# A gated attention and GeGLU kernel: the probabilities' product moved behind a down chain, and the ones' product moved behind the second sum

## The chip, the core and the metric

The kernel runs on one core of a Trainium2 chip. The metric is the device time of one execution in microseconds (us). Before the change three runs gave 1596.64, 1601.48 and 1602.04 us; the median is 1601.48 us.

TensorE is called PE below, VectorE DVE, ScalarE ACT, GpSimd POOL, and SyncE, which issues the transfers, SP.

## What is computed

For 2048 tokens of width 576, the output is a gated sum of two branches: `g * attention(x) + (1 - g) * ffn(x)`, with `g = sigmoid(x · gate_w)`.

- The attention branch has 32 heads of width 18 and works on four segments of 512 tokens. In each segment it takes a masked softmax of the scores and multiplies the probabilities by the values. It mixes this with what a running memory gives (a linear attention over the segments before), and the result goes through `wo`.
- The other branch is `(gelu(x @ w_gate) * (x @ w_up)) @ w_down`, with 4608 hidden columns. It is most of the work.

All of it is wanted in fp32 accuracy. The kernel writes each fp32 operand as two fp16 words, a high and a low one, and multiplies high by high, high by low and low by high.

## The kernel before

A first stage projects the queries, keys and values (up to about 255 us). Then comes a loop of 72 steps, `step(v)`, to about 1480 us, and last the product with `wo`.

The loop runs over 18 blocks `fb` of 256 hidden columns. A block takes four steps, `i4` = 0 to 3: two tiles `f` of 128 columns, each with the token pairs `p` = 0 and 1 (two segments of 512 tokens each). A step works out the gate sum and the up sum of its tile for two segments. It does so with fewer products than four, by a scheme of sums and differences: accumulators X in bank G, Y in bank U and V in bank V are filled by `product` and `rest`, copied and added by DVE, and end in `gelu` and `hidden`. In every block but the first, the steps with `i4` < 2 are the nested ones: their product into V is again split (`nest`, `nest_product`, `nest_last`), and its parts are spread over the step before.

Beside this, each step carries parts of other work:

- `chains` and `down`: the down products of the block before. A chain is six matmuls into a bank `dn`, over the two tiles of that block: hidden words (`hhr`, `hhd`) times the weight words `paird`. DVE adds the result to `acc` (line 1264). A step has eight chains, five `early` and three `late`.
- attention, two heads' halves a step: `scores` puts four score tiles into banks (tags `st`, `st`, `dn`, and `pv` or `dn`). DVE reads each with the mask and takes its maximum (line 1174, called by `put`). `powers` takes exponentials on ACT (line 1190), the high word on ACT (1191), the low word on POOL (1192), and has SP transpose both words by DMA into `pt`. `values` (line 1209) multiplies `pt` by the values: 20 small matmuls into bank `pv`.
- preparing the next weights: ACT makes high words, POOL low words. `low_d` (line 402) makes the low words of `paird` for a block in the last step of that block. `scales` multiplies the weights' sums of squares by a matrix of ones (two fp32 matmuls, line 94) and works out scales from them.

The order on PE, DVE, ACT and POOL is the order in which the code is written (`manual_schedule`); each engine runs its instructions in that order, and semaphores hold an instruction until its inputs are there and its output bank is free. The eight banks of PSUM are taken up by `dn` (two buffers), `st` (two), `pv`, V, G and U. A tag with two buffers hands them out in turn, so a third tile waits for the readers of the first.

At the end of a step stand `scores(2 * k + 1)`, whose last two tiles are both of tag `dn`, and, before a nested step, `nest(at, 3)`. The next step begins with `end_pair()`, in which DVE reads these two `dn` tiles, and then (lines 1454 to 1462):

```
            elif i4 < 2:
                if on(k - 2):
                    values(2 * k - 3)
                V, g1 = nested[fb, p], gl_tile()
            ...
            X, Y = bank("G"), bank("U")
            product(X, f, A11, x1, 0, 4, True)
```

Of the kernel before, what the change touches and what calls it, by code (L numbers as in the profile page):

```python
# [43 lines left out]
def kernel(ctx: ExitStack, tc: tile.TileContext, xs, wqk, wv, wo, wgu, wd, beta, out):  # L44
# [8 lines left out]
    def bank(tag, bufs=1, dt=F32):  # L53
        return ps.tile([P, 512 if dt == F32 else 1024], dt, name=tag, tag=tag, bufs=bufs)
# [36 lines left out]
    def sums(st, o=None):  # L91

        o = (spare() if o is None else o)[:, : st.shape[1]]
        pe.matmul(o, ones, st, start=True, stop=True)
        return o
# [168 lines left out]
    def scales(fb, o=None):  # L264

        o = sums(stat[fb % 2].rearrange("p a b -> p (a b)"), o)
        z = wts.tile([P, 6], F32, name="z", tag="z", bufs=2)
        dve.tensor_reduce(z[:, 4:6], o.rearrange("p (a b) -> p a b", a=2), AX.X, OP.add)
        dve.tensor_scalar(z[:, 0:4], x2, z[:, 4:5], 1e-30, OP.mult, OP.max)
        v = wts.tile([P, 2, 2], F32, name="v", tag="v", bufs=2)  # L270
        pb = wts.tile([P, 2, 4], F32, name="pb", tag="pb", bufs=3)
        dve.tensor_scalar(v[:, 0].bitcast(I32), z[:, 4:6].bitcast(I32), 1, EXP, OP.logical_shift_right, OP.bitwise_and)
        dve.tensor_scalar(pb[:, 0].bitcast(I32), z[:, 0:4].bitcast(I32), EXP, None, OP.bitwise_and)
        dve.tensor_scalar(v[:, 1].bitcast(I32), v[:, 0].bitcast(I32), EXP, None, OP.bitwise_xor)
        dve.tensor_scalar(pb[:, 1].bitcast(I32), pb[:, 0].bitcast(I32), EXP, None, OP.bitwise_xor)
        scl_a[fb] = v, pb

    def scales_out(fb):
        v, pb = scl_a.pop(fb)
        sc = wts.tile([P, 10], F32, name="sc", tag="sc", bufs=3)  # L280
        pool.tensor_scalar(sc[:, 0:2], v[:, 1], 2.0**-51, None, OP.mult)
        pool.tensor_scalar(sc[:, 2:6], xis, v[:, 0, 0:1], 2.0**50, OP.mult, OP.mult)
        pool.tensor_scalar(sc[:, 6:10], pb[:, 1], 2.0**14, None, OP.mult)
        pool.tensor_tensor(sc[:, 6:10], sc[:, 6:10], sc[:, 2:6], OP.mult)
        if fb:
            w = wts.tile([P, 4], F32, name="we", tag="we", bufs=2)
            pool.tensor_scalar(w, scl[fb - 1][1][:, 0], v[:, 0, 1:2], 2.0**35, OP.mult, OP.mult)
            ev = wts.tile([P, 16], F32, name="ev", tag="ev", bufs=2)
            pool.tensor_tensor(ev.rearrange("p (c q) -> p c q", c=4),
                               gate[:, 1].rearrange("p (c q) -> p c q", c=4),  # L290
                               w.unsqueeze(2).to_broadcast([P, 4, 4]), OP.mult)
            evs[fb - 1] = ev
        scl[fb] = (sc, pb)
# [167 lines left out]
    def nest_x(p):  # L461
        t = flat(kept["xt"][p][:, 8:15])
        return t[:, : 7 * HX], t[:, 7 * HX :]
# [13 lines left out]
    def nest_pairs_x(p, half):  # L477
        r, sc = sums_x[p][1, 2], xsc[:, 2 * p : 2 * p + 1]
        hi, lo = (t[:, 3 * HX :] for t in nest_x(p))
        if half == 0:  # L480
            act.activation(hi, r, AF.Copy, scale=sc)
        else:
            dve.scalar_tensor_tensor(lo, r, sc, hi, OP.mult, OP.subtract)
# [40 lines left out]
    def gl_tile():  # L524
        return mp2.tile([P, L], F32, name="gl", bufs=3)

    def product(o, f, a, x, h, l, start=False):

        w = pair_g[f]
        for k in range(2):  # L530
            for i, b in ((0, h), (0, l), (1, h)):
                pe.matmul(o, w[:, i, (a + k) * P : (a + k + 1) * P], x[:, b + k],  # L532
                          start=start and k == 0 and i == 0 and b == h, stop=k == 1 and i == 1,
                          skip_group_check=True)
# [3 lines left out]
    def first_product(v):  # L538
        f, p = divmod(v, 2)
        V = bank("pv" if v == 3 else "V")  # L540
        w = flat(s3_first["t"])
        for k, b in ((0, X00), (1, X10)):
            for i, j in ((0, 0), (0, 1), (1, 0)):
                a = (4 * i + 2 * f + k) * P
                x = nest_x(p)[j][:, b * HX : (b + 2) * HX]
                pe.matmul(V, w[:, a : a + P], x, start=k == i == j == 0, stop=k == i == 1, skip_group_check=True)
        if v == 3:
            s3_first.pop("t")
            hh_free.append(s3_first.pop("slot"))
        g1 = gl_tile()  # L550
        dve.tensor_copy(g1, V)
        return V, g1

    first, stay = ExitStack(), ctx.enter_context(ExitStack())
    with tc.tile_pool(name="prj", bufs=2, side="right", reuse_waits="tile") as pp:
# [135 lines left out]
        def vrows(s, q, b):  # L691
            x = x16[s]
            n = NH + 2 * b
            pv = bank("U") if (q, b) == (1, 0) else bank("dn", 2)
            chain_x(pv[:, :n], lambda i: x[:, i, q * P : (q + 1) * P], lambda k, i: W[9 + k][:, i, VB[b]])
            return pv, 2.0**-14, al[:, s, 1:2]
# [110 lines left out]
        with tc.manual_schedule(engines=ORDERED):  # L807
# [210 lines left out]
            for s in range(4):  # L1018
                p = s - 1
                if s:  # L1020
                    for q in range(4):
                        pv = vrows(s, q, 0)
# [14 lines left out]
                        pv = vrows(s, q, 1)  # L1037
# [67 lines left out]
    with tc.tile_pool(name="keep", bufs=2, side="right", reuse_waits="tile") as kp, ExitStack() as tail:  # L1105
# [91 lines left out]
        def values(a):  # L1197
            kk, e = divmod(a, 2)
            if e == 0:
                pvb[kk] = bank("pv")  # L1200
            o = pvb[kk]
            pr = turned_p.pop(a)
            v = vts[kk // 4]
            c0 = (kk % 4) * VC
            for qi in range(4):
                ov = o[:, (4 * e + qi) * VC : (4 * e + qi + 1) * VC]
                for kb in range(qi + 1):
                    for i in range(2):
                        pe.matmul(ov, pr[:, 10 * i + COL[qi] // P + kb], v[:, 4 * e + kb, c0 : c0 + VC],  # L1209
                                  start=kb == 0 and i == 0, stop=kb == qi and i == 1)  # L1210
# [19 lines left out]
        def result_high(gg):  # L1230
            ob = obs[gg]
            oh = ohs[gg] = ap_.tile([P, 8, 4 * DH], F16, name="oh", bufs=1)
            act.activation(flat(oh), flat(ob), AF.Copy, scale=wsc[:, 3:4])
# [32 lines left out]
        def chains(b, js):  # L1266
            for j in js:
                down(b, j // 2, j % 2)
                if j % 8 == 7:
                    for ff in (2 * b, 2 * b + 1):  # L1270
                        hp.pop((ff, j // 8))
                        hh_free.append(hh_slot.pop((ff, j // 8)))
                        if j == 31:
                            pair_d.pop(ff)
# [131 lines left out]
        def nest_last(b, V, p):  # L1406
            nest_product(b, V[:, HX : 2 * HX], WS4, X11, p)
# [20 lines left out]
        def step(v):  # L1428

            f, p = divmod(v, 2)  # L1430
            fb, i4 = divmod(v, 4)
            c, e = 2 * p, 2 * p + 1
            k = v - LAG
            on = lambda i: 0 <= i < 2 * H
            early = range(8 * i4, 8 * i4 + 5)
            late = range(8 * i4 + 5, 8 * i4 + 8)
            some = lambda b, js: chains(b, js) if b >= 0 else None
# [14 lines left out]
            if not fb:  # L1452
                V, g1 = ahead.pop(v) if v in ahead else first_product(v)
            elif i4 < 2:
                if on(k - 2):
                    values(2 * k - 3)
                V, g1 = nested[fb, p], gl_tile()
            else:
                V, g1 = bank("V"), holds[p]
                product(V, f, A22, x2_, 0, 4, True)  # L1460
            X, Y = bank("G"), bank("U")
            product(X, f, A11, x1, 0, 4, True)
            one = (2 if fb and i4 < 2 else 1) + (v == 4)
            if v == 4:
                dve.tensor_copy(Y, X)
                nest((1, 0), 2)
                some(0, early[:2])
                nest((1, 0), 3)
                some(0, early[2:3])
                nest_last(fb, V, p)  # L1470
                dve.tensor_copy(g1, V)  # L1471
                nest_pairs_x(1, 1)
            elif fb and i4 < 2:
                nest_last(fb, V, p)
                dve.tensor_copy(g1, V)
                dve.tensor_copy(Y, X)
                put(2 * k - 1, 3)
            else:
                put(2 * k - 1, 3)
                dve.tensor_copy(Y, X)  # L1480
# [5 lines left out]
                nest_pairs_x(v - 2, 0)  # L1486
            if v == 1:
                scale_result()
            some(fb - 1, early[3 * (v == 4) : one])
            put(2 * k - 1, 2)  # L1490
            puts.pop(2 * k - 1, None)
            if on(k - 2) and not (fb and i4 < 2):
# [62 lines left out]
                dve.tensor_tensor(g0, V, g0, OP.add)  # L1555
                gelu(f, c, g0, g0)
            put(2 * k, 0)
            some(fb - 1, early[3:])
            put(2 * k, 3)
            if fb and i4 == 1:  # L1560
                scales(fb + 1, bank("pv") if on(k) else None)
                scales_out(fb + 1)
            if on(k - 2) and not on(k):
                normalize(k - 2)
            if not fb:
# [7 lines left out]
            if done is not None:  # L1573
                result_high(done)
            product(Y, f, S4, x2_, 2, 6)
            if v == 3:
                nest(at, 1)
            rest(Y, f, UG, x2_, (0,) if fb else (0, 1))
# [184 lines left out]
        with tc.manual_schedule(engines=ORDERED):  # L1763
# [17 lines left out]
            fb = NB - 1  # L1781
# [88 lines left out]
```

## Time and profile before

| | |
|---|---|
| median of three runs | 1601.48 us |
| the profiled execution, its own time | 1598.08 us |
| its span | 1596.4 us |
| PE busy | 1564.9 us, 98% |
| DVE, ACT, POOL busy | 1249.5, 1208.7 and 1127.1 us |
| mean granted clock of PE | 0.996 |

PE is busy in nearly the whole span, so the time can only change where PE stands still or runs slower. A block of four steps takes some 74 us in the middle of the loop. The profile's timeline has one row for each group of like instructions, with the start, the duration, the engine, the line, and, in brackets, how long the engine had been idle before it and what released it. Where matmuls follow each other, the duration of a group contains the draining of its last one; the next group's start tells when PE could go on.

### The profile page before, as it was taken

To read this page: it belongs to the slowest core of one execution; us is meant where nothing else is said; L and a number is where in the kernel's file an instruction comes from. 1 tells how busy PE (TensorE), PEld (TensorE's weight loads), DVE (VectorE), ACT (ScalarE), POOL (GpSimd) and SP (SyncE) were. 2 spreads that over 40 slices of the span, in tenths; PEclk is the share of its full clock that TensorE was granted. 3 is DMA by queue.
4 is the path that set the end of the run, shared out by engine and by line. 5 is a ranking of instruction groups with operands and counts; after the bars stand their busy time and mean duration, and the time that the engine had idled before them with its cause. 6 is when DMAs were issued, how large, how long until landed. Compare 5 with 4: busy or idle time off the path is not lost.

```text
span 1596.4 us, 33958 instructions
## 1 busy us (share of the span) xinstructions
PE 1564.9 (98%) x12220; PEld 955.9 (60%) x12220; DVE 1249.5 (78%) x3254; ACT 1208.7 (76%) x2059; POOL 1127.1 (71%) x1220
## 2 busy tenths in 40 slices
PE   9999999999999999999999999999999999999999
PEld 5665655565555555556655555665555556656577
DVE  6788976778787788878887878888778888787665
ACT  7567544888888888888888888888878888787421
POOL 4345555877786858686786777776858686777597
PEclk9999999999999999999999999999999999999999
DMA  6534331676867767777767887868678767764546
GB/s 232 211 126 134 123 116 56 114 140 120 151 122 143 132 117 132 133 131 133 128 125 127 122 142 125 145 125 156 133 118 136 130 137 137 130 113 96 119 82 172
DMA packets 472833, 209.97 MB, mean 132 GB/s; under 512 B 427688, under 2 KB 437416, under 8 KB 472152
## 3 DMA queue, kind: packets, MB, share of 16 engines
q1 hardware_dynamic: 472664, 207.80, 65.5%
q8 instruction: 96, 1.57, 0.4%
q14 instruction: 73, 0.60, 0.1%
HBM read 91.87 MB, written 27.26 MB: 75 GB/s over the span
## 4 chain that ended last, share of the span: by engine, by line
PE 76%; DMA 7%; POOL 6%; DVE 5%; ACT 4%; issue 2%; SPq 0%; ACTq 0%; DVEq 0%; POOLq 0%
PE dn L1256 19%; PE U L532 14%; PE G L532 10%; PE V L532 5%; DMA pt<-pb 5%; PE pv L1209 4%; PE V L1377 3%; PE st L412 3%; PE dn L419 2%; POOL pb L1192 2%; PE U L1302 2%; PE U L412 1%; PE G L412 1%; PE V L1307 1%; PE st L1171 1%
## 5 line engine op out<-in xcount | busy, mean ns | idle before, releaser
L1192 POOL TENSOR_TENSOR pb<-pb,ph 128x896 f16<-128x896 f32 (+1 forms) x256 | 368.4, 1439 | 278.4 <-ACT ph L1191 268.4
L532 PEld LDWEIGHTS <-pairg 128*128 128x128 f16 x2592 | 248.5, 98 | 260.5 <-issue 14.8
L1256 PE MATMUL dn<-paird,hhr 128*128 128x288 f16 x2115 | 330.1, 287 | 0.1
L1190 ACT ACTIVATE pb<-pb,mb,esc 128x512 f32<-128x512 f32 (+3 forms) x512 | 305.0, 642 | 5.5 <-issue 0.4
L1264 DVE SCALAR_TENSOR_TENSOR acc<-dn,ev,acc 128x288 f32<-128x288 f32 x533 | 262.4, 512 | 41.5 <-PE dn L1256 35.7
L1256 PEld LDWEIGHTS <-hhr 128*128 128x128 f16 x2160 | 208.2, 98 | 80.3 <-issue 11.8
L532 PE MATMUL G<-x,pairg 128*128 128x512 f16 x864 | 212.5, 382 | 1.3 <-DVE gl L1279 1.2
L1256 PE MATMUL dn<-paird,hhd 128*128 128x288 f16 x1275 | 210.0, 286 | 0.6 <-DVE acc L1264 0.6
L532 PE MATMUL U<-xt,pairg 128*128 128x512 f16 x864 | 209.9, 379 | 0.0
L1191 ACT ACTIVATE ph<-pb 128x896 f16<-128x896 f32 (+1 forms) x256 | 188.5, 736 | 8.1
L345 POOL TENSOR_TENSOR pairg<-raw,pairg 128x384 f16<-128x384 f32 (+2 forms) x144 | 157.6, 1116 | 17.3 <-ACT pairg L341 17.3
L1174 DVE CUSTOM_DVE_ANT_0 pb<-st,mask 128x512 f32<-128x512 f32 (+1 forms) x256 | 156.9, 613 | 1.1 <-DMA pt<-pb 1.1
L1256 PEld LDWEIGHTS <-hhd 128*128 128x128 f16 x1296 | 124.7, 98 | 52.4 <-issue 7.5
L1174 DVE CUSTOM_DVE_ANT_0 pb<-dn,mask 128x256 f32<-128x256 f32 (+1 forms) x192 | 67.1, 374 | 91.3 <-PE dn L1171 89.6
L1185 ACT ACTIVATE mb<-mx,esc 128x4 f32<-128x4 f32 x128 | 36.8, 287 | 98.3 <-DVE mx L1174 98.3
L1377 PE MATMUL V<-xt,nest 128*128 128x256 f16 x714 | 106.7, 274 | 0.3 <-DVE hold L1401 0.2
L532 PE MATMUL U<-x,pairg 128*128 128x512 f16 x432 | 104.9, 379 | 0.1
L532 PE MATMUL V<-x,pairg 128*128 128x512 f16 x426 | 103.9, 380 | 0.9 <-DVE gl L1471 0.9
L1209 PE MATMUL pv<-vt,pt 128*128 128x37 f16 x2560 | 87.4, 179 | 15.1 <-DMA pt<-pb 14.0
L1209 PEld LDWEIGHTS <-pt 128*128 128x128 f16 x2560 | 83.4, 96 | 24.1 <-DMA pt<-pb 16.3
L1297 ACT ACTIVATE gl<-gl,sc 128x512 f32<-128x512 f32 x110 | 75.7, 715 | 28.5 <-DVE gl L1550 16.7
L1377 PEld LDWEIGHTS <-nest 128*128 128x128 f16 x714 | 65.0, 98 | 33.1 <-issue 10.8
(369 smaller groups left out, 3114.8 us busy)
## 6 DMA issues: line engine op xcount, KB each, us to landing
raw<-in_wgu_dram SPq DMA_DIRECT2D x36, 640.0 KB
rawd<-in_wd_dram SPq DMA_DIRECT2D x36, 288.0 KB
qt<-qk SPq DMA_DIRECT2D x132, 72.0 KB
kt<-qk SPq DMA_DIRECT2D x132, 72.0 KB
qk<-stage SPq DMA_DIRECT2D x36, 256.0 KB
qt<-qk SPq DMA_DIRECT2D x132, 36.0 KB
kt<-qk SPq DMA_DIRECT2D x132, 36.0 KB
vp<-vstage SPq DMA_DIRECT2D x16, 296.0 KB
```

The costliest lines, as they stand in the source:

```text
L345: pool.tensor_tensor(spot(f, *p, 1), raw_g[f][:, p[0] : p[1]], spot(f, *p, 0), OP.subtract)
L412: pe.matmul(o, w(k, a), x[:, i], start=n == 0, stop=n == 13, skip_group_check=True)
L532: pe.matmul(o, w[:, i, (a + k) * P : (a + k + 1) * P], x[:, b + k], start=start and k == 0 and i == 0 and b == h, stop=k == 1 and i == 1, ...
L1174: dve.tensor_tensor_reduce(scored(a, qi), out[qi], mask[:, L - (qi + 1) * P :], 1.0, -3e38, OP.add, OP.max, mx[a][:, qi : qi + 1])
L1190: act.activation(r, r, AF.Exp, bias=b[:, qi : qi + 1], scale=esc[:, 0, c : c + 1])
L1191: act.activation(h[:, cols], p, AF.Copy)
L1192: pool.tensor_tensor(low[:, cols], p, h[:, cols], OP.subtract)
L1209: pe.matmul(ov, pr[:, 10 * i + COL[qi] // P + kb], v[:, 4 * e + kb, c0 : c0 + VC], start=kb == 0 and i == 0, stop=kb == qi and i == 1)
L1256: pe.matmul(o[:, :NH], hh[:, a, q * P : (q + 1) * P], w[:, b, n * NH : (n + 1) * NH], start=i == 0, stop=i == 5)
L1264: dve.scalar_tensor_tensor(av, o[:, :NH], ev, av, OP.mult, OP.add)
L1297: act.activation(t, o, AF.Gelu_apprx_tanh, scale=scl[f // 2][0][:, 2 + c : 3 + c])
L1377: pe.matmul(o, w[:, (7 * c + i) * P : (7 * c + i + 1) * P], x[d], start=start and n == 0, stop=n == 2, skip_group_check=True)
```

## The change

In the nested steps `values` moves from the head of the step to a place behind X's product, the last nested product and the two copies. The first down chain of the step takes its place at the head. So the order on PE goes from `values`, G's product, last nested product, two chains to chain, G's product, last nested product, `values`, chain.

In the steps with `i4` = 1, `scales` with the ones' product moves from before the product into Y (S4) to behind it. In step 4, the first nested one, one chain moves forward and the bounds of the others follow.

```diff
             elif i4 < 2:
-                if on(k - 2):
-                    values(2 * k - 3)
                 V, g1 = nested[fb, p], gl_tile()
+                if v != 4:
+                    some(fb - 1, early[:1])
             else:
                 V, g1 = bank("V"), holds[p]
                 product(V, f, A22, x2_, 0, 4, True)
@@
                 nest_last(fb, V, p)
                 dve.tensor_copy(g1, V)
                 nest_pairs_x(1, 1)
+                some(0, early[3:4])
             elif fb and i4 < 2:
                 nest_last(fb, V, p)
                 dve.tensor_copy(g1, V)
                 dve.tensor_copy(Y, X)
                 put(2 * k - 1, 3)
+                if on(k - 2):
+                    values(2 * k - 3)
             else:
@@
-            some(fb - 1, early[3 * (v == 4) : one])
+            if v != 4:
+                some(fb - 1, early[1 if fb and i4 < 2 else 0 : one])
@@
-            some(fb - 1, early[3:])
+            some(fb - 1, early[3 + (v == 4) :])
             put(2 * k, 3)
-            if fb and i4 == 1:
-                scales(fb + 1, bank("pv") if on(k) else None)
-                scales_out(fb + 1)
@@
             product(Y, f, S4, x2_, 2, 6)
+            if fb and i4 == 1:
+                scales(fb + 1, bank("pv") if on(k) else None)
+                scales_out(fb + 1)
             if v == 3:
                 nest(at, 1)
```

What the change does on PE, at two places. The first is the passage into a nested step with `i4` = 1, before: two score tiles into `dn`, the nested product into V (`nest`), the probabilities `pt` times the values `vt`, the product into G, and further on the first down chain.

```order
L1171 MATMUL dn<-kt,qt 128x256
...
L1171 MATMUL dn<-kt,qt 128x128
...
L1377 MATMUL V<-xt_2333,nest 128x256
...
L1209 MATMUL pv<-vt,pt 128x37
...
L532 MATMUL G<-x_1132,pairg 128x512
...
L1256 MATMUL dn<-paird,hhd_11124 128x288
```

And now, at the same place:

```order
L1171 MATMUL dn<-kt,qt 128x256
...
L1171 MATMUL dn<-kt,qt 128x128
...
L1377 MATMUL V<-xt_2333,nest 128x256
...
L1256 MATMUL dn<-paird,hhd_11124 128x288
...
L532 MATMUL G<-x_1132,pairg 128x512
...
L1209 MATMUL pv<-vt,pt 128x37
```

The chain has come forward by 20 matmuls of `values`, six into G and three into V. It is now the third tile of tag `dn` with only three nested matmuls between it and the two score tiles.

The second place is the ones' product, in the same step. Before, it stands between a down chain (`dn`) and the product into bank U:

```order
L1256 MATMUL dn<-paird,hhr_11684 128x288
L94 MATMUL pv<-stat_88,ones 128x10
L532 LDWEIGHTS pairg
L532 MATMUL U<-x_1750,pairg 128x512
...
L1302 LDWEIGHTS pairg
L1302 MATMUL U<-x_1750,pairg 128x512
```

Now it stands behind the six matmuls of that product and ahead of the one of line 1302, which closes it:

```order
L1256 MATMUL dn<-paird,hhr_11684 128x288
L532 LDWEIGHTS pairg
L532 MATMUL U<-x_1750,pairg 128x512
...
L94 MATMUL pv<-stat_88,ones 128x10
L1302 LDWEIGHTS pairg
L1302 MATMUL U<-x_1750,pairg 128x512
```

The fp32 product into `pv` has moved back by six matmuls of 512 columns.

## Rows read from the trace of the kernel before

**Rows 1.** The page: busy time, share of the span and instructions of PE

```profile
PE 1564.9 (98%) x12220; PEld 955.9 (60%) x12220; DVE 1249.5 (78%) x3254; ACT 1208.7 (76%) x2059; POOL 1127.1 (71%) x1220
```

**Rows 2.** Waits of PE over the span: line and releaser, total us, times, longest

```profile
PE pv L1209 <- DMA pt<-pb: 14.0, 15, 2.5
PE pv L94 <- DVE mx L1174: 7.1, 16, 0.4
...
PE pv L1209 <- DMA pt<-ph: 1.1, 2, 0.9
```

**Rows 3.** Timeline of PE at the head of a first nested step

```profile
702.59 0.50 PE L1377 MATMUL V<-xt,nest 128*128 128x256 f16 x3
703.01 0.19 PE L1209 MATMUL pv<-vt,pt 128*128 128x37 f16 x1
704.08 0.64 PE L1209 MATMUL pv<-vt,pt 128*128 128x37 f16 x19 [0.88 <-DMA pt<-pb]
704.57 1.46 PE L532 MATMUL G<-x,pairg 128*128 128x512 f16 x6
705.86 0.49 PE L1377 MATMUL V<-xt,nest 128*128 128x256 f16 x3
```

**Rows 4.** Timeline of PE at the head of the second nested step

```profile
722.96 0.50 PE L1377 MATMUL V<-xt,nest 128*128 128x256 f16 x3
723.30 0.67 PE L1209 MATMUL pv<-vt,pt 128*128 128x37 f16 x20
723.81 1.46 PE L532 MATMUL G<-x,pairg 128*128 128x512 f16 x6
```

**Rows 5.** Timeline of DVE at the head of the second nested step

```profile
723.53 0.41 DVE L1404 TENSOR_TENSOR hold<-V,hold 128x256 f32<-128x256 f32 x1
723.86 0.41 DVE L1174 CUSTOM_DVE_ANT_0 pb<-dn,mask 128x256 f32<-128x256 f32 x1
724.20 0.08 DVE L1174 DVE_READ_ACCUMULATOR2_ANT mx<- 128x1 f32 x1
```

**Rows 6.** Timeline at the head of step 5: DVE, then PE

```profile
275.18 0.75 DVE L1279 SCALAR_TENSOR_TENSOR gl<-G,sc,gl 128x512 f32<-128x512 f32 x1
...
275.98 1.45 PE L532 MATMUL G<-x,pairg 128*128 128x512 f16 x6 [0.20 <-DVE gl L1279]
```

**Rows 7.** Timeline of POOL: low words of the down weights, two of 16 blocks

```profile
702.51 2.53 POOL L402 TENSOR_TENSOR paird<-rawd,paird 128x576 f16<-128x576 f32 x2
...
1376.72 2.52 POOL L402 TENSOR_TENSOR paird<-rawd,paird 128x576 f16<-128x576 f32 x2
```

**Rows 8.** Timeline around the ones' product: DVE, then PE

```profile
734.61 0.69 DVE L1550 TENSOR_TENSOR gl<-U,gl 128x512 f32<-128x512 f32 x1
...
736.25 0.36 PE L94 MATMUL pv<-stat,ones 128*128 128x10 f32 x2 [0.45 <-DVE mx L1174]
...
736.46 1.46 PE L532 MATMUL U<-x,pairg 128*128 128x512 f16 x6
```

**Rows 9.** Timeline behind the ones' product: ACT, then POOL

```profile
739.93 0.30 ACT L1185 ACTIVATE mb<-mx,esc 128x4 f32<-128x4 f32 x1 [1.34 <-DVE mx L1174]
...
744.01 3.48 POOL L1192 TENSOR_TENSOR pb<-pb,ph 128x896 f16<-128x896 f32 x2 [3.91 <-ACT ph L1191]
```

**Rows 10.** Stretches: us, busy of PE, PEld, DVE, ACT, POOL, granted clock, DMA

```profile
927.00:933.00 6.00, 4.14 (x46) 2.33 (x45) 3.00 (x10) 5.86 (x11) 5.25 (x4) 1.00 0.96 259
...
554.30:558.00 3.70, 3.67 (x29) 1.91 (x30) 0.00 (x0) 2.59 (x6) 3.39 (x3) 0.55 0.78 247
853.20:858.50 5.30, 5.29 (x41) 3.27 (x42) 2.27 (x5) 2.97 (x6) 4.62 (x4) 0.68 1.52 258
1154.20:1159.40 5.20, 5.20 (x40) 3.09 (x41) 1.65 (x3) 2.40 (x5) 5.02 (x4) 0.67 1.46 229
```

**Rows 11.** Timeline of PE in the first of these stretches

```profile
929.37 0.19 PE L1209 MATMUL pv<-vt,pt 128*128 128x37 f16 x1 [0.92 <-DMA pt<-ph]
930.50 0.64 PE L1209 MATMUL pv<-vt,pt 128*128 128x37 f16 x19 [0.94 <-DMA pt<-pb]
```

## What the change will do to the time

> **What bounds the kernel now.** The busy times come first: PE is busy 98% of the span [rows 1], the other engines 71 to 78%. The matmuls are the same before and after, so only PE's waits and its clock can move the time. The list of PE's waits comes next [rows 2]: 14.0 us in 15 waits and 1.1 us in 2 are `values` waiting for the transposed probabilities, and 7.1 us in 16 are the ones' product waiting for bank `pv`. These are the waits that the change aims at. The third view is the timeline at the places that move. At the head of a first nested step (`i4` = 0) one matmul of `values` runs, the other 19 wait 0.88 us for the transfer of the low words, and G's product starts behind them [rows 3]. At the second nested step (`i4` = 1) nothing waits as a rule: the nested product starts at 722.96, `values` at 723.30 and G's product at 723.81 [rows 4]. So three nested matmuls take 0.34 us and `values` takes 0.51. Of the waits for transfers 13 heads of first nested steps hold nearly all, three have none.
>
> **What goes.** Four items.
> - The transfer waits. Moved behind the chain, six matmuls into G (704.57 to 705.86, 1.29 us) and three into V (0.33), `values` starts over 2.3 us later in PE's work, and later still by the new waits below. The longest wait is 2.5 us [rows 2], so all of them should go: 15.1 us, and about 0.16 more for each of the 15, since the wait is counted from the end of the first matmul's 0.19 us although the next one would follow it after 0.03 (0.49 us for 19, [rows 3]). That is 17.5 us.
> - The ones' product. It waits 0.45 us for DVE to read the score tile in `pv` [rows 8]. The product into U, which now goes first, needs U read by DVE: line 1550 ends at 735.30, and PE was ready at 735.80 (736.25 less 0.45). So U's product runs at once and covers the wait: it takes 1.29 us, and `pv` was free before 736.25. 7.1 us go. What is late next: the scales come some 0.8 us later on DVE, which then stands before work that waits for PE anyway.
> - The slow clock behind the three longest transfer waits (2.1 to 2.5 us). Behind them PE's granted clock is 0.55 over 3.70 us, 0.68 over 5.30 and 0.67 over 5.20 [rows 10], so 0.45 × 3.70 + 0.32 × 5.30 + 0.33 × 5.20 = 5.1 us are lost there, which come back if no such wait is left.
> - At step 5 G's product waited 0.2 us for DVE [rows 6]; the chain now stands there. 0.2 us.
> Together 17.5 + 7.1 + 5.1 + 0.2 = 29.9 us.
>
> **What comes.** The chain at the head has two new waits, since PE runs matmuls in order and G's product, the last nested one and `values` queue behind it.
> - Its bank. `dn` has two buffers, and both were filled by the scores just ahead. The first comes free when DVE has taken the maximum of the 256-column tile. At the second nested step that is 724.28 (724.20 + 0.08; [rows 5]). DVE cannot be earlier: in front of it stand the sum of the last nested product (723.53) and the work on G, both behind PE. A release takes about 0.05 us: line 1279 ends at 275.93 and PE goes at 275.98 [rows 6]. So the chain starts at 724.33 instead of 723.30: 1.03 us of standing still, where 0 was. In the heads of the other blocks this read of the tile also begins 0.9 us behind the nested product's start (here 723.86 against 722.96), so the wait is the same. 16 second nested steps (blocks 1 to 16) have it: 16.5 us. From below it is 0 (the tile free in time), from above some 1.2 us (the release as slow as that of the ones' product: 0.15 us).
> - Its weights. In a first nested step the chain is the first to use the low words of `paird`, which POOL makes at the end of the block. POOL does both from 702.51 to 705.04 [rows 7], and the nested product starts at 702.59 [rows 3]: the second low word is ready 2.45 us behind that start. The chain's fifth matmul needs it. The sixth follows; two of six matmuls of a 0.73 us chain take 0.25. So G's product starts at 2.45 + 0.05 + 0.25 = 2.75 us, where 0.34 + 0.73 = 1.07 is pure work: 1.65 to 1.7 us of standing still, the bank's 1.03 included. In 13 of 16 heads POOL starts these words 0 to 0.1 us ahead of the nested product (two of the 13 are in [rows 7]); in three it starts 0.5 to 0.8 us ahead, and the wait is about 1.1. 13 × 1.65 + 3 × 1.1 = 24.8 us.
> Together 41.3 us. Before, this chain stood 1.6 us behind G's start, and POOL was done in time.
>
> Do the later heads mend this? POOL and ACT work without a pause from the time at which ACT gets the maxima behind the ones' product: there ACT waited 1.34 us for DVE and POOL then 3.91 us for ACT [rows 9], so both start from PE's time, not from their own backlog. Waits of PE ahead of that point push POOL back by as much, so its lag at the next head stays.
>
> **The sum.** 41.3 − 29.9 = +11.4 us. The profiled execution took 1598.08 us, which gives 1609.5; I say 1609 us. It lies 3.4 us under the median of 1601.48; I do not add these, since what varies most is the transfer waits, which go. Against the median 1609 is +0.5%, just where a measurement of this kernel begins to tell a change (0.5% is taken as the bound: under 1593.5 is faster, over 1609.5 slower). The range of the unknown costs: with the slow release (+0.12 on 16 and 1 us over the other heads) 1612; with DVE's reading 0.4 us sooner 1602. The forecast's own range is 1603 to 1616.
>
> **A rule on the clock.** After the waits of 2.1 to 2.5 us the clock fell to the lower level (1.2 GHz) for some us; after two waits of 0.92 and 0.94 us with one small matmul between [rows 11] it stayed at 1.00 [rows 10]. The chain's two waits, 1.03 and some 0.65 us with four matmuls between, are nearer to the second case, so the sum has no loss for them. The Trainium skill (TensorE: Matmul & The Clock Gate, section "A second HAM failure mode: psum-queue depth-cycling") says that a PE that idles briefly between groups of matmuls while it cycles through PSUM banks can swing between half and full clock, and loses throughput by it. That speaks against this change; by the rule each first nested head would go slow, and the last rival below would be the likeliest. The trace so far shows such swings only behind longer waits.
>
> **Rivals.**
> - The bank is free in time. If DVE, with an addition fewer behind the head, runs 1.03 us ahead at the end of a step, the bank's wait goes: 16.5 us less, and 0.5 less in the three heads, while POOL's low words still hold the 13 heads. 41.3 − 18 − 29.9 = −6.6: 1591 us, faster. For it: DVE is busy only 78%. Against it: the reads ahead of the tile wait for PE's own last matmuls [rows 5]. It decides once DVE is over 0.7 us earlier. 8%.
> - POOL is ready sooner. If its lag is made up, say because PE's new waits give it time, only the bank holds: 32 × 1.03 = 33.0, less 29.9: 1601 us, no change. Against it: [rows 9]. 14%.
> - The ones' product gains nothing: its wait goes but the later scales delay POOL or the next weights by as much. Then 7.1 us stay: 1616 us. For it: POOL takes the scales in order. Against it: the pause of 3.91 us behind them [rows 9]. 8%. A form of this is that the change doesn't do what it says, and `values` still waits behind the chain; with 2.3 us more ahead of it and the longest wait 2.5, that is a part of 1% or so.
> - The clock falls at each first nested head, 1.7 us a time as in [rows 10] (5.1 by three): 13 × 1.7 = 22 us: 1631 us. Half of them: 1620. 10%.
> - The forecast, 60%. Some of it lies on either side of 1609.5.
>
> **How the numbers follow.** Slower: half of the forecast's 60, 8 and 10, together 47%. No change: the other half (28 to 30) and the 14, about 43%. Faster: the 8, and a little of the tail of the second rival: 10%. The range from 1597 to 1622 leaves out the first rival and the full form of the clock's.
>
> **What would show it.** In the waits of PE a new line, `dn` of line 1256 behind DVE's maximum (`mx`, line 1174), some 30 times with about 1 us each, and another, `dn` behind POOL's `paird`, some 13 times with about 0.65; the lines of 1209 and 94 gone; granted clock 1.00 in every stretch. G's product should start 2.1 us behind the nested product's start in second nested steps and 2.75 in first ones. The forecast is wrong if the line behind DVE is missing or far shorter than 0.8 us a time, or if the clock falls behind the chains.

## The result

Eight runs of the changed kernel took 1605.12 us in the median (1604.87 to 1607.04), eight of the kernel before 1599.35 us (1596.06 to 1602.04). The ratio is 1.0039, with a 95% interval from 1.0027 to 1.0051: slower by 6 us. The median lies inside the 0.5% that the prediction took as the bound of no change; the upper end of the interval lies just on it. The profiled execution has a span of 1603.2 us where the one before had 1596.4.

The list of PE's waits after the change (line and releaser, us in total, times, longest):

```profile
PE dn L1256 <- DVE mx L1174: 27.8, 32, 0.9
PE dn L1256 <- POOL paird L402: 6.9, 14, 0.5
```

The three lines of [rows 2] are gone: `values` and the ones' product wait no more. In their place stand the two that were forecast, the head chain's bank 32 times and its weights 14 times. Their sum is 34.7 us; the three that went made 22.2.

The head of a first nested step after, PE (start, us, engine, line, idle before it and its releaser), to be held against [rows 3]:

```profile
704.97 0.50 PE L1377 MATMUL V<-xt,nest 128*128 128x256 f16 x3
706.34 0.53 PE L1256 MATMUL dn<-paird,hhr 128*128 128x288 f16 x3 [0.87 <-DVE mx L1174]
706.71 0.28 PE L1256 MATMUL dn<-paird,hhd 128*128 128x288 f16 x1
707.48 0.41 PE L1256 MATMUL dn<-paird,hhd 128*128 128x288 f16 x2 [0.48 <-POOL paird L402]
707.72 1.46 PE L532 MATMUL G<-x,pairg 128*128 128x512 f16 x6
```

POOL at that place:

```profile
704.91 2.51 POOL L402 TENSOR_TENSOR paird<-rawd,paird 128x576 f16<-128x576 f32 x2
```

Four matmuls of the chain run at 706.34, then the fifth waits for POOL, whose second low word ends at 707.42. G's product starts 2.75 us behind the nested product, 1.68 more than the work between them (0.34 + 0.73).

The head of the second nested step after, PE and then DVE:

```profile
725.88 0.50 PE L1377 MATMUL V<-xt,nest 128*128 128x256 f16 x3
727.25 0.53 PE L1256 MATMUL dn<-paird,hhr 128*128 128x288 f16 x3 [0.87 <-DVE mx L1174]
...
727.98 1.46 PE L532 MATMUL G<-x,pairg 128*128 128x512 f16 x6
```

```profile
726.78 0.41 DVE L1174 CUSTOM_DVE_ANT_0 pb<-dn,mask 128x256 f32<-128x256 f32 x1
727.12 0.08 DVE L1174 DVE_READ_ACCUMULATOR2_ANT mx<- 128x1 f32 x1
```

DVE is done with the tile at 727.20, and the chain starts at 727.25. PE was ready at 726.22, so it stands still for 1.03 us, at a place where nothing waited in [rows 4].

The ones' product, before and after. First the chain ahead of it in the kernel before (the rows that follow are in [rows 8]):

```profile
735.27 0.53 PE L1256 MATMUL dn<-paird,hhd 128*128 128x288 f16 x3
```

And the changed kernel:

```profile
739.22 0.53 PE L1256 MATMUL dn<-paird,hhd 128*128 128x288 f16 x3
739.59 1.46 PE L532 MATMUL U<-x,pairg 128*128 128x512 f16 x6
740.88 0.29 PE L94 MATMUL pv<-stat,ones 128*128 128x10 f32 x2
741.02 0.38 PE L1302 MATMUL U<-x,pairg 128*128 128x512 f16 x1
```

Three of the chain's matmuls take 0.37 us. So before, PE could have gone on at 735.64, but it ran the ones' product at 736.25 and U's product at 736.46: 0.82 us. Now U's product follows the chain at once, and the ones' product takes 0.14. That is 0.68 us less per block, and the starts give the same in all 16 blocks.

The clock, in the blocks that had been slow, and one other (us, busy of PE, PEld, DVE, ACT, POOL, granted clock, DMA):

```profile
555.00:563.00 8.00, 6.64 (x56) 3.85 (x55) 6.14 (x16) 6.03 (x11) 7.03 (x6) 1.00 1.20 223
704.97:712.00 7.03, 5.68 (x54) 3.53 (x52) 5.17 (x14) 5.52 (x9) 6.21 (x5) 1.00 1.03 270
1156.00:1164.00 8.00, 6.63 (x60) 3.90 (x60) 6.05 (x17) 6.10 (x10) 7.19 (x7) 1.00 1.25 246
```

The stretches at 0.55 to 0.68 of [rows 10] have no counterpart in the profiled execution, whose mean granted clock is 1.000.

### The profile page after: what moved, and what is told of

It is laid out like the page before. It is cut to its first block, busy times and chain, and to the rows that moved or that the text cites. A ratio compares the mean times of both kernels' runs of the same rounds, so it can differ in the third digit from the quotient of the medians.

```text
span 1603.2 us, 33958 instructions
## 1 busy us (share of the span) xinstructions
PE 1559.9 (97%) x12220; PEld 955.2 (60%) x12220; DVE 1257.4 (78%) x3254; ACT 1208.8 (75%) x2059; POOL 1123.7 (70%) x1220
## 4 chain that ended last, share of the span: by engine, by line
PE 62%; POOL 12%; DVE 3%; ACT 3%; issue 1%; POOLq 0%; ACTq 0%; DVEq 0%
PE dn L1256 20%; PE U L532 14%; PE G L532 9%; PE V L532 5%; PE pv L1209 3%; PE V L1377 3%; POOL paird L402 2%; POOL pairg L345 2%; POOL pb L1192 2%; PE U L1302 1%; PE V L1307 1%; DVE gl L1279 1%; POOL x L1707 1%; PE V L1302 1%; POOL pairg L1690 1%
```

## The experiments

The theory: the head chain meets two separate lags, DVE's reading of the `dn` tile and POOL's low words. Both hold PE, while the move of `values` and that of the ones' product each do what they are for. The rivals: the two lags are one; the cost is in the later place of `values` or in the chain's addition ahead of DVE's copies; the ones' product gains less, or nothing. All seven kernels were timed beside the kernel before, which gave 1598.45 us (17 runs) beside the first four and 1598.54 (11 runs) beside the last three.

**The ones' product alone moved** (the kernel before otherwise):

```diff
             put(2 * k, 3)
-            if fb and i4 == 1:
-                scales(fb + 1, bank("pv") if on(k) else None)
-                scales_out(fb + 1)
...
             product(Y, f, S4, x2_, 2, 6)
+            if fb and i4 == 1:
+                scales(fb + 1, bank("pv") if on(k) else None)
+                scales_out(fb + 1)
```

> The kernel before with the ones' product alone moved behind the second sum's last product. Theory: PE's stop at the ones' product was really 0.61 us (0.45 in the list of waits and 0.16 that the draining of the chain ahead hides) and goes in all 16 blocks, with 0.07 us of the product itself: 0.68 x 16 = 10.9 us less than before, about 1588.5 us. Rival (my sum on record): only the listed 0.45 us go, 7.1 us less, 1592 us. Rival 2: the later scales hold POOL or DVE up and eat the gain, 1599 us.

Measured: 1589.71 us, ratio 0.9946 (0.993 to 0.9962). The later scales do not eat the gain: 1599 is ruled out. Its list of waits:

```profile
PE pv L1209 <- DMA pt<-pb: 17.5, 17, 2.4
...
PE pv L1209 <- DMA pt<-ph: 1.2, 2, 0.6
```

The ones' line is gone, but `values`, still at the head, waits 3.6 us more than in [rows 2]. By the starts of G's product, six second nested heads stand still for 0.9 to 1.8 us each, where two did before, for 0.3 and 0.7. With one profile of each kernel it is not shown whether the later scales do this or the transfers vary by themselves. So the time, between the theory's 1588.5 and the 1592 of the rival, does not tell them apart by itself; the next one does.

**`values` alone moved** (the changed kernel with the ones' product at its old place):

```diff
             put(2 * k, 3)
+            if fb and i4 == 1:
+                scales(fb + 1, bank("pv") if on(k) else None)
+                scales_out(fb + 1)
...
             product(Y, f, S4, x2_, 2, 6)
-            if fb and i4 == 1:
-                scales(fb + 1, bank("pv") if on(k) else None)
-                scales_out(fb + 1)
```

> The changed kernel with the ones' product put back to its old place; the chain at the head and the later place of values stay. Theory: the list of waits shows the ones' line again with 7.1 us beside the two lines of the down chain (27.8 and 6.9 us), and the time is 10.9 us over the changed kernel: 1616 us, 1.1% over the kernel before. Rival: if the move of the ones' product gave only 7.1 us, 1612 us.

Measured: 1616.57 us, ratio 1.0116 (1.0099 to 1.0133). It is 11.5 us over the changed kernel's 1605.12, near to 0.68 × 16 = 10.9 and not to 7.1. (The kernel before was 0.9 us quicker beside this run than beside the changed kernel, so the difference is not smaller than that.) The list:

```profile
PE dn L1256 <- DVE mx L1174: 27.8, 32, 0.9
PE pv L94 <- DVE mx L1174: 7.2, 16, 0.4
PE dn L1256 <- POOL paird L402: 7.1, 14, 0.7
```

The chain's two waits do not depend on the ones' product.

**The chain behind G's product**, `values` as in the changed kernel:

```diff
-                if v != 4:
-                    some(fb - 1, early[:1])
...
             elif fb and i4 < 2:
+                some(fb - 1, early[:1])
                 nest_last(fb, V, p)
```

> The changed kernel with the step's first down chain taken from the head and put behind G's product; values stays behind the last nested product. Theory (the chain's bank and its weights are late at the head): both waits of the chain go, since it comes 1.6 us later; G's product now meets DVE's work on G, which ends 0.3 us behind the nested product's end, 32 heads x 0.3 = 9 us, and a first nested head may keep 0.1 us for POOL's low words. 42 - 9 - 2 = 31 us less than the changed kernel: about 1574 us. Rival (it is the later place of values, or the chain's addition ahead of DVE's two copies, that costs): nothing gained beside the changed kernel, 1600 us or more.

Measured: 1575.06 us, ratio 0.9857 (0.9841 to 0.9874). The chain's addition still stands ahead of DVE's copies, and `values` still stands behind the last nested product, so neither is what costs. What is left is the wait that was foretold for G's product, 0.36 us by the starts at each of 32 heads (0.20 in the list):

```profile
PE G L532 <- DVE gl L1279: 7.6, 35, 0.6
...
PE dn L1256 <- POOL paird L402: 0.4, 1, 0.4
```

**POOL's low words of the down weights first**, the changed kernel otherwise:

```diff
+            if i4 == 3:
+                for f in (n0, n0 + 1):
+                    low_d(f)
             low_g(n0 + 1 + i4 // 2, i4 % 2)
-            if i4 == 3:
-                for f in (n0, n0 + 1):
-                    low_d(f)
```

> The changed kernel with POOL's two low words of the down weights made ahead of the low words of the gate and up weights in a block's last step, 2.0 us sooner; nothing moves on PE or DVE. Theory: the chain's wait for POOL (6.9 us in 14) goes, the wait for the bank (27.8 us in 32) stays as it is: 13 first nested heads go from 1.68 to 1.03 us, 8.5 us less than the changed kernel, about 1596.5 us. Rival: if the bank and POOL were one lag, both lines would shrink, or neither.

Measured: 1595.78 us, ratio 0.9981 (0.9969 to 0.9992). POOL's line is gone and DVE's is the same to the tenth, so the lags are two:

```profile
PE dn L1256 <- DVE mx L1174: 27.8, 32, 0.9
```

**The bank free sooner**, the changed kernel otherwise: the `dn` tiles are made first, and DVE reads the first of them ahead of its work on G.

```diff
-            for qi, r, *tags in PIECES:
+            for qi, r, *tags in PIECES[2:] + PIECES[:2] if e else PIECES:
...
-                    for qi in (1, 0):
+                    for qi in (0,) if len(g) > 4 else (1, 0):
...
                 ends.append((f, c, X, g0))
-                if at:
-                    end_first()
             if on(k):
                 puts[2 * k + 1] = scores(2 * k + 1)
+                if fb and at:
+                    puts[2 * k + 1](1)
+            if fb and at:
+                end_first()
```

> The changed kernel, in which the scores of the second head half are made with the two dn tiles first, and DVE takes the maximum of the first of them ahead of its work on G (two DVE instructions change places); the chain stays at the head. Theory of two separate lags (bank and POOL): the bank comes free about 0.1 us behind the nested product's end in place of 1.03, so the 16 second nested heads lose 0.9 us each and the three first heads without a lag of POOL too, 17 us in all; the other 13 still wait for POOL's low words until 2.5 us. About 1588 us, and the wait list shows DVE's line nearly gone and POOL's grown to some 1.6 us a time, 20 us. Rival (the chain at the head is late for another reason than this tile): DVE's line stays near 28 us and the time near 1605.

Measured: 1592.05 us, ratio 0.9956 (0.9944 to 0.9968). DVE's line has left the list, and POOL's has grown as expected. A first nested head:

```profile
700.79 0.50 PE L1377 MATMUL V<-xt,nest 128*128 128x256 f16 x3
701.33 0.28 PE L1256 MATMUL dn<-paird,hhr 128*128 128x288 f16 x1
702.12 0.40 PE L1256 MATMUL dn<-paird,hhr 128*128 128x288 f16 x2 [0.51 <-POOL paird L402]
702.37 0.28 PE L1256 MATMUL dn<-paird,hhd 128*128 128x288 f16 x1
703.36 0.40 PE L1256 MATMUL dn<-paird,hhd 128*128 128x288 f16 x2 [0.71 <-POOL paird L402]
703.61 1.46 PE L532 MATMUL G<-x,pairg 128*128 128x512 f16 x6
```

```profile
PE dn L1256 <- POOL paird L402: 18.2, 30, 0.7
```

The chain starts 0.54 us behind the nested product's start, and POOL holds its second and its fifth matmul: G's product starts at 2.82 us, no sooner than the 2.75 of the changed kernel. In second heads the still time fell from 1.03 to 0.20 us: 16 × 0.83 = 13.3, which gives 1591.8. One of them:

```profile
721.77 0.50 PE L1377 MATMUL V<-xt,nest 128*128 128x256 f16 x3
722.30 0.53 PE L1256 MATMUL dn<-paird,hhr 128*128 128x288 f16 x3
...
723.04 1.46 PE L532 MATMUL G<-x,pairg 128*128 128x512 f16 x6
```

The expectation was 4 us too low: it took 0.9 a second head in place of 0.83, and it counted on three first heads in which POOL has no lag. None of the 16 first heads gained more than 0.04; the two with the shortest wait stand still for 1.36 and 0.99 us, where it was 1.28 and 1.03.

**Both**, the edits of the last two together:

> The same as the one with the bank free sooner, and POOL makes the low words of the down weights first, 2.0 us sooner. Theory: both lags are gone, so the two gains are more than their sum alone (17 and 9 us): the 13 first heads now drop from 1.68 us to about 0.1. 42.5 - 32 x 0.12 = 38.6 us less than the changed kernel: about 1566.5 us, no line of the chain's over 4 us in PE's waits. Rival: if the lags were one, 1605 - 17 - 9 = 1579 us at best.

Measured: 1571.70 us, ratio 0.9829 (0.9814 to 0.9843), the best of all. That is 33 us under the changed kernel, where the two gains by themselves are 9.3 and 13.1. In a first head both lags hold the chain, so undoing one leaves the other in force; only with both undone does it go on. A head, first and second alike:

```profile
713.71 0.50 PE L1377 MATMUL V<-xt,nest 128*128 128x256 f16 x3
714.25 0.53 PE L1256 MATMUL dn<-paird,hhr 128*128 128x288 f16 x3
...
714.98 1.46 PE L532 MATMUL G<-x,pairg 128*128 128x512 f16 x6
```

PE is ready at 714.05 and goes at 714.25: 0.20 us a head (0.09 at one of the 32), 6.3 in all against 42.5 in the changed kernel. Of the 36.2 us between these, 33.4 show in the time; that is 5 us less than the 38.6 expected, half of it because 0.20 stays at a head and not 0.12. Of the other 2.8 us, the trace shows 1.2 at two places where the nested product waits for DVE, such as this one, where the chain ahead of it was done by 490.73 (490.36 and 0.37):

```profile
490.36 0.53 PE L1256 MATMUL dn<-paird,hhd 128*128 128x288 f16 x3
491.35 0.49 PE L1377 MATMUL V<-xt,nest 128*128 128x256 f16 x3 [0.46 <-DVE hold L1393]
```

The remaining 1.6 were not traced.

**G finished sooner**, on the kernel with the chain behind G's product:

```diff
+            sooner = fb and i4 == 0
+            if sooner:
+                low_rests(f, (X, U4, x1), (Y, UG, x2_))
+                ends.append((f, c, X, g0))
+                end_first()
+                nest(at, 2)
             if on(k - 1):
                 values(2 * k - 2)
-            if v != 3:
+            if v != 3 and not sooner:
                 nest(at, 2)
...
-            if fb:
+            if fb and not sooner:
```

> The kernel with the chain behind G's product, in which, ahead of a second nested step, X is finished and DVE works on G before the nested sums, and values of the same step goes behind them. Theory: of the 0.36 us that G's product waits for DVE at each of 32 heads, the 16 second ones go, 5.8 us: about 1569.5 us. Rival: DVE then waits for ACT's gelu or the nested sums come late, and nothing is gained: 1575 us.

Measured: 1572.66 us, ratio 0.9834 (0.982 to 0.9849). The list shows that the second heads' wait has gone:

```profile
PE G L532 <- DVE gl L1279: 4.2, 18, 0.6
```

But only 2.4 of the 5.8 us show in the time. The trace places most of the other 3.4: from a first head to the second one PE takes 19.83 us in the median, where it took 19.63 in the kernel with the chain behind G's product, and 16 × 0.20 = 3.2. In that step the half-height matmuls of `low_rests` (64 rows, `64*128`) now stand between full ones:

```profile
711.70 0.53 PE L1256 MATMUL dn<-paird,hhd 128*128 128x288 f16 x3
712.16 0.39 PE L1307 MATMUL G<-x,pairg 64*128 64x512 f16 x1
712.16 0.39 PE L1307 MATMUL U<-x,pairg 64*128 64x512 f16 x1
712.48 0.83 PE L1377 MATMUL V<-xt,nest 128*128 128x256 f16 x6
713.15 0.67 PE L1209 MATMUL pv<-vt,pt 128*128 128x37 f16 x20
713.75 0.39 PE L1171 MATMUL st<-kt,qt 54*128 54x512 f16 x2
```

The chain was done at 712.07, so the half-height pair starts 0.09 late. The pair takes 0.22 where the scores follow it, and 0.32 here; and the scores (54 rows) start 0.09 behind `values`, which takes 0.51. Where the pair stood just ahead of the scores, there was one such gap of 0.10 in place of three. What makes the gaps was not tried.

## Why the prediction was nearly right

1609 was forecast and 1605.12 measured, in the range; the way was right, slower. The size was 11.4 us by the sum, and came out as 6.8 in the profiled executions and 5.8 in the medians, which put the result on the near side of the 0.5% line (the 43% case, not the 47% one). By the steps:

- The bank. Right: 1.03 us forecast, 1.03 measured, in all 16 second heads, 16.5 us. The kernel that reads the tile sooner shows that this tile is the cause.
- The weights. Right: 1.65 us a first head forecast, 1.67 to 1.73 measured, in 14 heads in place of 13; with the two others (1.28 and 1.03) it is 26.0 us in place of 24.8. The kernel with POOL's order changed shows the cause. POOL's lag stays from block to block, as argued from [rows 9]: in these heads it starts its words 0 to 0.07 us ahead of the nested product.
- The transfer waits. Right, and a little under-sized: 17.5 forecast. By the starts of G's product against the work ahead of it, heads of the kernel before stood still 18.6 us, of which the change left none.
- The ones' product. This is the term that was most mis-sized: the step "7.1 us go". The listed wait of 0.45 us was taken as the whole. The list counts from the modelled end of the chain ahead, which lies 0.16 us behind the point at which the next matmul could have started. The prediction added this 0.16 to the transfer waits and left it out here. (It left it out at step 5 too: G's product stood still there for 0.36 us by the starts, not 0.2.) With 0.07 us that the ones' product itself takes less behind matmuls of 512 columns, it is 0.68 a block: 10.9 us, as the kernel with `values` alone moved confirms.
- The clock. Right for the profiled execution: full in every stretch, with 32 waits listed as 0.87 us and 14 as some 0.5 at the heads. Two of the eight runs of the changed kernel show a mean granted clock of 0.998, with 1606.54 and 1607.04 us; what lowered it in them is not on record. The Trainium skill (TensorE: Matmul & The Clock Gate, section "A second HAM failure mode: psum-queue depth-cycling") says that a PE that idles briefly between groups of matmuls while it cycles through PSUM banks swings between half and full clock. The profiled execution does not agree: its mean granted clock is 1.000.

The sum with the measured terms: 42.5 come, 18.6 + 10.9 + 5.1 + 0.4 = 35.0 go, +7.5 us; 6.8 were measured. The 0.7 between them was not traced. The forecast came as near as it did partly by luck: 1.2 us more came than it had, and 5.1 more went, and these two misses take from each other.

The rivals: the bank was not free in time, and POOL did not catch up; the kernel with the bank free sooner comes near to the first rival, 1592 us where 1591 had been said. That this agrees so well is partly luck: the rival took 18 us off for the bank, and 13.3 went, while the ones' product gave 3.8 more than its sum had. The rival was right in one thing: a change of places of a few DVE and POOL instructions decides whether this change is worth −1.7% or +0.4%.

## What to carry to other kernels

Work that is put at a head as a cover must be ready there itself: list for its first instruction each bank, each weight word and the engine that gives it last, and the time at which that engine is done, before counting the wait that it is to cover. Where two late releases hold the same place, undo both; either alone gained 9 and 13 us here, both together 33. And count a wait from the time at which the next matmul could have started, not from the list, where 0.16 us a time were missing here.

## What was not expected of the hardware

The time became steadier than it had been: 1604.87 to 1607.04 us after against 1596.06 to 1602.04 before, and 1571.57 to 1572.16 in the best kernel. In the profile of the kernel before, the waits for transfers run from 0.2 to 2.5 us; after the change, the chain's wait for DVE is the same 0.87 us at 32 heads of 32. The granted clock varies with the time. Of the 28 runs of the kernel before beside the experiments, the quickest took 1593.52 us at a mean granted clock of 1.000 and the slowest 1605.85 at 0.994. As an estimate from these, 0.006 × 1600 = 9.6 of the 12.3 us between them are the lower clock itself. That the long transfer waits bring the low clock in these runs too is not shown, since a trace is kept of one run only; in that one, all three falls stand behind such waits [rows 10].
